# A new order list for the first fourteen steps of an attention and two-layer kernel, with two halves scaled on another engine and a split last tile

## The chip, the cores and the metric

The kernel runs on one core of a Trainium2 chip. The metric is the time of one execution on the device, in microseconds. The core has five engines that work side by side, each with its own queue of instructions that it takes in order: PE (TensorE, matrix products), DVE (VectorE), ACT (ScalarE), POOL (GpSimd) and SP (SyncE, which here only issues DMAs). An engine that waits for a semaphore holds up everything behind it in its queue.

## The reference

Attention over local windows and block summaries, and then two dense layers with a rational function between them:

```python
# B, H, S, D = 4, 8, 768, 64; blocks of 32 keys, window of 16
k_sum = k.reshape(B, H, nb, block, D).max(axis=3)
v_sum = v.reshape(B, H, nb, block, D).mean(axis=3)
scores_l = scale * np.matmul(q, k.transpose(0, 1, 3, 2))      # kept where |i - j| < 16
scores_s = scale * np.einsum('bhsd,bhnd->bhsn', q, k_sum) + np.log(block)
a = softmax(concatenate([scores_l_masked, scores_s]))
x = (a @ concatenate([v, v_sum])) as [3072, 512]
h = x @ w_in                                                  # [3072, 2048]
g = (a0 + a1 h + a2 h^2 + a3 h^3) / (1 + |b0| |h| + |b1| h^2 + 1e-6)
out = g @ w_out                                               # [3072, 512]
```

## The kernel before

**Halves.** The queries are cut into 48 "halves" of 64 positions (all 8 heads of one batch); a half sees a window of 96 keys and 24 block sums, 120 columns for each of four pairs of heads. A half goes through a chain of small stages: its key sums are copied beside its keys (DVE, tile `kw`, halves 8, 9, 12 and 13 of the first sixteen), PE makes the scores (`sc`), DVE adds the mask and takes the extreme of each row (`ss`, `sm`), ACT takes four exponentials and their sums, DVE a reciprocal, POOL multiplies the four pairs by it (tile `ss`), PE transposes (`pt`), ACT or DVE copies the transposed tile out (`pts`; `ENG_P` says which), PE multiplies by the values (`av`), ACT or DVE casts the result (`xh`; `ENG_X`) and DVE keeps the rest of the cast (`xl`). `PAIRS` says which neighbours have their scores made in one interleaved run of products. Halves 0 to 7 are the first group's 512 tokens and are all needed before the first dense step; 8 to 15 are the second group's.

**Steps.** Six groups of 512 tokens go through 16 slices of the hidden layer each: 96 steps. A step is 12 products of PE into a bank `h` (first layer, every operand as a high and a low part), the rational function on ACT, DVE and POOL (`gelu`, parts a to k, tiles `ta`, `tq`, `tu`, `gh`, `gl`), and 12 products into the four banks `po` (second layer). `h` and the transposed tiles of early halves share two PSUM banks. Weights arrive packed (`wr`) and are split into a high and a low part in up to six stages `w` over ACT, POOL and DVE; the first eight slices stay in `wearly`.

**The order written out.** Up to step 13 the order of all engines is a text, `TEXT`, of 562 tokens. Each token stands for the next stage of one chain: `h7` the next stage of half 7, `w3` of the splitting of weights 3, `x2` four of step 2's first-layer products, `y2` three of its second-layer products, `ga2` to `gk2` the parts of its rational function, `K`, `k` key loads and key sums of batch 0, `I`, `i` those of batch 1, `Q` queries, `V` value windows, `A` queries and keys of a half, `W` a load of packed weights, `F`, `G` values for the block means, `v`, `u` the products that make the means, `m`, `n` their copies, `S` constants. The class `Kept` ties each instruction to the one before it on its engine, so that every engine runs its instructions in the order in which the text emits them. From step 14 on a loop takes over, in which the framework's own scheduler orders the engines; there every step has its 12 products of each layer, and every fourth step two halves.

**The end.** `finish` copies the four `po` banks of a group out. For the last bank of the last group ACT copies the left half and DVE the right half into one tile `o`, and two DMAs, from ACT's and SP's queues, write it.

Nearly all instructions are emitted through `call` in `Kept`, and so have line 109 in the profile; they are told apart by their tiles.

Of the kernel before, what the change touches and what calls it, by code (L numbers as in the profile page):

```python
# [8 lines left out]
F32 = mybir.dt.float32  # L9
# [4 lines left out]
ALU = mybir.AluOpType  # L14
# [7 lines left out]
NT, DM, DFF = B * S, H * D, 2048  # L22
P = 128
NPAIR = H // 2
# [6 lines left out]
NK = NKW + NB  # L31
# [5 lines left out]
HPG = GT // HQ  # L37
# [7 lines left out]
LAG = 3  # L45
SOFF = 12
NWARM = 6
TEXT = ("K0 K2 k0 K1 Q0 k1 k2 K3 k3 S0 Q1 F0 W0 V0 V1 V2 A9 V3 V5 V6 V7 W1 V4 W2 W3 h0 A8 G0 h0 h0 h1 h1 h0 h3 h1 h2 h0 h4 h6 h1 h2 h4 v0 h5 h0 h1 h1 h3 h4 h2 h0 h3 h6 h2 h2 h0 h2 "
# [11 lines left out]
AVGW = NK + NB - 4  # L60
NLATE = 4
NSTG = 8
# [2 lines left out]
CROSS = 1  # L65
OWN = (0, 1)
NTA = NTQ = NTU = 2
PAIRS = "11001000"
SMODE = "xxxxxxxxxxxxxxxx"
ENG_P = "dddddaadaaaaaaaa"  # L70
ENG_X = "daadaaaaaaadaaaa"
MODE = "ccccceceeccccccc"
SQ_PS = "001001001001110"
PRODUCT = "00000000000000"
TREE = "0000"
KDMA = "00000000"
NHALF = NT // HQ


# [1 line left out]
def tile_kernel(ctx, tc, qw_in, kraw, kwin, vpad, vred, wio, a, b, cmask, cident, cavg, out):  # L81
# [9 lines left out]
    gp = ctx.enter_context(tc.tile_pool(name="gp", bufs=3))  # L91
# [27 lines left out]
    pe, dve, act, gps, syn = (Kept(e) for e in (nc.tensor, nc.vector, nc.scalar, nc.gpsimd, nc.sync))  # L119
# [153 lines left out]
    def softmax(jj, sc):  # L273

        bi, j = divmod(jj, NJ)
        mt = mask[:, 0 if j == 0 else (2 if j == NJ - 1 else 1), :]
        pool, tag = (gp, "gl") if jj < HPG and jj % 2 else (pp, "p")
        ss = pool.tile([P, NPAIR, P], F32, tag=tag, name=f"ss{jj}")[:, :, 0:NK if jj < 2 * HPG else P]
        sm = sp.tile([P, 2, NPAIR], F32, tag="sm", name=f"sm{jj}")
        for pr in range(NPAIR):  # L280
            dve.tensor_tensor_reduce(
                out=ss[:, pr, 0:NK], in0=sc[:, pr * NK:(pr + 1) * NK], in1=mt, op0=ALU.add, op1=ALU.min,
                scale=-SCALE, scalar=3.0e38, accum_out=sm[:, 0, pr:pr + 1])
        yield
        ahead = jj < 2 * HPG and SMODE[jj] == "y"
        if ahead:
            gps.tensor_tensor(ss, ss, sm[:, 0, :].unsqueeze(2).to_broadcast([P, NPAIR, NK]), op=ALU.subtract)
        if jj < 2 * HPG:
            yield
        if ahead:  # L290
            act.activation(ss, ss, AF.Exp, scale=-1.0)
            yield
            dve.tensor_reduce(sm[:, 1, :], ss, axis=AX.X, op=ALU.add)
            dve.tensor_scalar_add(sm[:, 1, :], sm[:, 1, :], 1e-9)
        else:
            for pr in range(NPAIR):
                act.activation(ss[:, pr, 0:NK], ss[:, pr, 0:NK], AF.Exp, scale=-1.0,
                               bias=sm[:, 0, pr:pr + 1], accum_out=sm[:, 1, pr:pr + 1])
            act.activation(sm[:, 1, :], sm[:, 1, :], AF.Copy, bias=1e-9)
            yield  # L300
        dve.reciprocal(sm[:, 1, :], sm[:, 1, :])
        yield
        if jj >= 2 * HPG:
            gps.memset(ss[:, :, NK:], 0.0)
        for pr in range(NPAIR):
            gps.tensor_scalar(ss[:, pr, 0:NK], ss[:, pr, 0:NK], sm[:, 1, pr:pr + 1], 1.0, op0=ALU.mult, op1=ALU.mult)
        att[jj] = ss

# [2 lines left out]
    def half(jj):  # L311

        other = jj ^ 1
        pair = PAIRS[jj // 2] == "1"
        if jj >= HPG:
# [272 lines left out]
    def finish(g, po):  # L588
        for t in range(TPG):
            if g == NG - 1:  # L590
                o = gp.tile([P, DM], F32, tag="gl" if t % 2 else "gh", name=f"o{g}_{t}")
            else:
                o = (gp if t in OWN else pp).tile([P, DM], F32, tag="o" if t in OWN else "p", name=f"o{g}_{t}", bufs=2 if t in OWN else 4)
            if g == NG - 1 and t == TPG - 1:
                rows = out[g * GT + t * P:g * GT + (t + 1) * P, :]
                act.copy(o[:, 0:DM // 2], po[t][:, 0:DM // 2])
                dve.tensor_copy(o[:, DM // 2:], po[t][:, DM // 2:])
                act.dma_start(out=rows[:, 0:DM // 2], in_=o[:, 0:DM // 2])
                syn.dma_start(out=rows[:, DM // 2:], in_=o[:, DM // 2:])
                continue  # L600
            if g == NG - 1 and t % 2:
                dve.tensor_copy(o, po[t])
            else:
                act.copy(o, po[t])
            syn.dma_start(out=out[g * GT + t * P:g * GT + (t + 1) * P, :], in_=o)
# [107 lines left out]
    for step in range(NSTRICT, NG * NFC + LAG):  # L713
        g, fc = divmod(step, NFC)
# [85 lines left out]
```

## Time and profile before

| | us |
|---|---|
| median of 3 runs | 642.72 |
| lowest, highest | 640.96, 643.12 |
| the profiled execution | 643.12 |
| its span from first to last instruction | 641.3 |
| busy in the span: PE, DVE, ACT, POOL | 619.3, 569.2, 459.7, 254.7 |

In lines of the timeline the columns are start and length in us, engine, operation, tile written and tiles read, shapes, count, and in brackets the idle time just before and what ended it. In lines of groups the columns after the count are the total busy time in us and the mean of one in ns, then the idle time before them with its main causes. Matmuls are pipelined, so their lengths overlap: twelve products of 512 columns follow each other in 2.72 us.

### The profile page before, as it was taken

What the parts mean: (1) busy time and instruction counts of PE and PEld (TensorE: products, weight loads), DVE (VectorE), ACT (ScalarE), POOL (GpSimd) and SP (SyncE); (2) the same over time, 40 slices, a digit from 0 to 9 for tenths busy, and PEclk for the clock granted to TensorE, in tenths of its full rate; (3) what the DMA queues carried; (4) which work ended last, traced back from release to release, by engine and by line L of the source; (5) the groups of instructions that cost most, each with busy time, mean ns of one, the idle gap of its engine ahead of it and who ended that gap; (6) DMA issues with size and microseconds to landing.
All of it is one profiled execution on the core that took longest, in us unless ns stands there. A gap on an engine that the chain in (4) does not pass through costs nothing.

```text
span 641.3 us, 11876 instructions
## 1 busy us (share of the span) xinstructions
PE 619.3 (97%) x4068; PEld 495.4 (77%) x4068; DVE 569.2 (89%) x1152; ACT 459.7 (72%) x1032; POOL 254.7 (40%) x353
## 2 busy tenths in 40 slices
PE   8797899999999999999999999999999999999997
PEld 5565667778778887888888878888888888888886
DVE  5689989999989999988988989988988989898884
ACT  3987989978778667777667687676786675755553
POOL 1838567574243244243243234334234232222221
PEclk9998999999999999999999999999999999999999
DMA  9997756604434424333424342322342210100001
GB/s 322 301 351 259 219 169 195 230 26 132 135 136 146 125 86 138 114 130 108 143 83 133 106 151 86 103 90 84 92 151 83 73 64 1 46 20 2 0 2 65
DMA packets 52136, 78.58 MB, mean 123 GB/s; under 512 B 6132, under 2 KB 33396, under 8 KB 50156
## 3 DMA queue, kind: packets, MB, share of 16 engines
q1 hardware_dynamic: 50796, 75.67, 36.0%
q0 software_dynamic: 560, 1.77, 1.5%
q8 instruction: 32, 0.52, 0.4%
q10 hardware_dynamic: 720, 0.38, 0.2%
q14 instruction: 28, 0.23, 0.1%
HBM read 61.31 MB, written 14.73 MB: 119 GB/s over the span
## 4 chain that ended last, share of the span: by engine, by line
PE 46%; DVE 28%; ACT 13%; issue 6%; POOL 5%; DMA 2%; DVEq 0%; ACTq 0%; POOLq 0%
PE po L109 21%; PE h L109 20%; DVE tu L109 9%; DVE tq L109 8%; DVE gh L109 4%; ACT ta L109 4%; POOL ss L109 3%; ACT ss L109 3%; PE sc L109 2%; PE av L109 2%; DVE ss L109 2%; DMA kres<-in_kraw_dram 1%; ACT tu L109 1%; DVE tb L109 1%; DVE ks L109 1%
## 5 line engine op out<-in xcount | busy, mean ns | idle before, releaser
L109 POOL TENSOR_TENSOR gl<-tu,ta 128x512 fp32r<-128x512 f32 x96 | 130.0, 1354 | 300.9 <-DVE tu L109 163.0
L109 ACT ACTIVATE ta<-tq,cs 128x512 f32<-128x512 f32 x96 | 69.6, 725 | 91.7 <-DVE tq L109 91.4
L109 PE MATMUL po<-wearly,gh 128*128 128x512 f32 x384 | 121.1, 397 | 1.0 <-ACT o L109 1.0
L109 POOL TENSOR_SCALAR ss<-ss,sm 128x120 f32<-128x120 f32 x192 | 93.8, 506 | 65.8 <-DVE sm L109 64.7
L109 PE MATMUL po<-w,gh 128*128 128x512 f32 x384 | 119.8, 393 | 0.0
L109 PE MATMUL h<-xh,wearly 128*128 128x512 f32 x384 | 98.3, 395 | 0.5 <-ACT xh L109 0.5
L109 PE MATMUL h<-xh,w 128*128 128x512 f32 x384 | 96.4, 390 | 1.3 <-DVE tu L109 0.7
L109 PEld LDWEIGHTS h<-xh,wearly 128*128 128x128 f32 x384 | 72.3, 189 | 16.7 <-issue 0.7
L109 PEld LDWEIGHTS h<-xh,w 128*128 128x128 f32 x384 | 71.8, 188 | 16.9 <-ACT ta L109 1.1
L109 PEld LDWEIGHTS po<-wearly,gh 128*128 128x128 f32 x384 | 70.4, 188 | 18.6 <-ACT o L109 2.9
L109 DVE SCALAR_TENSOR_TENSOR gh<-tu,cs,ta 128x512 fp32r<-128x512 f32 x96 | 73.3, 763 | 11.7 <-ACT ta L109 1.9
L109 PEld LDWEIGHTS po<-w,gh 128*128 128x128 f32 x384 | 71.1, 188 | 15.7 <-issue 1.3
L109 ACT ACTIVATE ss<-ss,sm 128x120 f32<-128x120 f32 x192 | 73.3, 386 | 11.2 <-DVE sm L109 11.0
L109 PE MATMUL po<-wearly,gl 128*128 128x512 f32 x192 | 74.9, 390 | 0.0
L109 PE MATMUL po<-w,gl 128*128 128x512 f32 x192 | 74.8, 390 | 0.0
L109 DVE SCALAR_TENSOR_TENSOR tu<-tu,cs,tq 128x512 f32<-128x512 f32 x96 | 72.3, 753 | 2.7
L109 ACT ACTIVATE tu<-h,cs 128x512 f32<-128x512 f32 x96 | 74.7, 778 | 0.0
L109 DVE SCALAR_TENSOR_TENSOR tu<-tu,cs,h 128x512 f32<-128x512 f32 x96 | 71.1, 740 | 2.2
L109 DVE SCALAR_TENSOR_TENSOR tq<-tq,gh 128x512 f32<-128x512 f32 x96 | 67.4, 702 | 2.8
L109 ACT ACTIVATE ta<-h,cs 128x512 f32<-128x512 f32 x96 | 65.3, 680 | 3.7 <-POOL gl L109 3.5
L109 DVE TENSOR_TENSOR tu<-tu,h 128x512 f32<-128x512 f32 x96 | 64.9, 676 | 1.2 <-ACT tu L109 0.7
L109 ACT ACTIVATE ta<-ta 128x512 f32<-128x512 f32 x96 | 60.7, 633 | 2.7
(76 smaller groups left out, 905.5 us busy)
## 6 DMA issues: line engine op xcount, KB each, us to landing
wr<-in_wio_dram SPq DMA_DIRECT2D x15, 1024.0 KB
cross<-tb SPq DMA_DIRECT2D x32, 256.0 KB
vw<-in_vpad_dram SPq DMA_DIRECT2D x42, 192.0 KB
kw<-in_kwin_dram SPq DMA_DIRECT2D x40, 192.0 KB
pts<-cross SPq DMA_DIRECT2D x96, 64.0 KB
out_dram<-o SPq DMA_DIRECT2D x23, 256.0 KB
qw<-in_qw_dram SPq DMA_DIRECT2D x40, 128.0 KB
kr<-in_kraw_dram SPq DMA_DIRECT2D x12, 384.0 KB
```

The costliest lines, as they stand in the source:

```text
L109: out = getattr(self.engine, name)(*args, **kw)
```

## The change

It puts another text in place of `TEXT`, with the same 562 tokens in another order, and changes five settings and two places of code.

- `PAIRS`: halves 6 and 7 make their scores in one run too.
- `SMODE`: half 1 goes the way "y": POOL subtracts the extreme from all four pairs in one instruction, ACT takes one exponential over 480 columns, DVE sums it and adds the small constant; its four scalings stay on POOL. Halves 3 and 5 go the new way "z": DVE scales all four pairs in one product with the reciprocal broadcast, in place of POOL's four.
- `ENG_P`: the transposed tiles of halves 5 and 14 are copied by DVE instead of ACT. `ENG_X`: half 3's cast goes from DVE to ACT, half 10's from ACT to DVE.
- `KDMA`: half 12's key sums are copied by a DMA from SP's queue instead of by DVE (the other mark in the text stands at half 11, which copies none).
- The last output tile's right half gets a tile of its own.

```diff
-PAIRS = "11001000"
-SMODE = "xxxxxxxxxxxxxxxx"
-ENG_P = "dddddaadaaaaaaaa"
-ENG_X = "daadaaaaaaadaaaa"
+PAIRS = "11011000"
+SMODE = "xyxzxzxxxxxxxxxx"
+ENG_P = "ddddddadaaaaaada"
+ENG_X = "daaaaaaaaaddaaaa"
...
-KDMA = "00000000"
+KDMA = "00011000"
...
-        for pr in range(NPAIR):
+        if jj < 2 * HPG and SMODE[jj] == "z":
+            dve.tensor_tensor(ss, ss, sm[:, 1, :].unsqueeze(2).to_broadcast([P, NPAIR, NK]), op=ALU.mult)
+        for pr in range(NPAIR) if jj >= 2 * HPG or SMODE[jj] != "z" else ():
             gps.tensor_scalar(ss[:, pr, 0:NK], ss[:, pr, 0:NK], sm[:, 1, pr:pr + 1], 1.0, op0=ALU.mult, op1=ALU.mult)
...
+                o2 = gp.tile([P, DM], F32, tag="gh", name=f"o{g}_{t + 1}")
                 act.copy(o[:, 0:DM // 2], po[t][:, 0:DM // 2])
-                dve.tensor_copy(o[:, DM // 2:], po[t][:, DM // 2:])
+                dve.tensor_copy(o2[:, 0:DM // 2], po[t][:, DM // 2:])
                 act.dma_start(out=rows[:, 0:DM // 2], in_=o[:, 0:DM // 2])
-                syn.dma_start(out=rows[:, DM // 2:], in_=o[:, DM // 2:])
+                syn.dma_start(out=rows[:, DM // 2:], in_=o2[:, 0:DM // 2])
```

Of the order itself, engine by engine, the places of which the prediction speaks (a number after a point is the stage of the chain; in a half's chain .1 is the scores, .5 the reciprocal, .6 the scaling, .7 the transposes, .8 the copy, .9 the product with the values, .10 the cast, .11 the rest of the cast; in `w` .0 is ACT's conversion, .2 DVE's combine, .4 DVE's subtraction):

```
PE, before:  ... h4.1 h6.1 v0 h5.1 h0.7 v1 v2 v3 h7.1 v4 v5 h3.7 h2.7 h1.7 h0.9 ...
PE, after:   ... h4.1 h6.1 (and half 7) v0 h0.7 v1 h5.1 v2 v3 h3.7 v4 v5 h2.7 h0.9 h1.7 ...
PE, before:  ... x5 y2 y2 y2 h10.7 y2 h10.9 x6 x6 x6 h12.1 y3 x7 y3 h11.7 ...
PE, after:   ... x5 y1 y2 x6 y2 x6 y2 x6 h10.7 h10.9 y2 y3 x7 x7 h12.1 y3 h11.7 ...
ACT, before: ... h7.4 h2.10 h1.10 h5.8 w1.0 h5.10 h6.8 h4.10 h6.10 h7.10 w1.3 w2.0 w3.0 ga0 ...
ACT, after:  ... h7.4 h2.10 h1.10 w1.0 h3.10 h5.10 h6.8 h4.10 w2.0 h7.10 h6.10 w1.3 ga0 gb0 w2.3 w3.0 ...
DVE, before: ... ge1 gc1 gf1 h8.5 i0 w3.4 gi1 w4.2 ge2 gc2 gj1 i1 h9.5 gf2 w4.4 gi2 w5.2 h8.11 gj2 ...
DVE, after:  ... ge1 gc1 w3.4 gf1 h8.5 i0 gi1 ge2 w4.2 gc2 gj1 h9.5 gf2 i1 w4.4 w5.2 gi2 h8.11 gj2 ...
DVE, before: ... h10.5 i3 h9.11 w6.4 gi4 w7.2 gj4 h12.0 ge5 gc5 gf5 h11.5 h10.11 w8.2 gi5 gj5 ...
DVE, after:  ... h10.5 i3 w6.4 gi4 h9.11 gj4 w7.2 ge5 gc5 h11.5 gf5 h10.10 h10.11 w8.2 gi5 gj5 ...
SP, before:  K0 K2 K1 Q0 K3 Q1 F0 W0 V0 V1 V2 A9 V3 V5 V6 V7 W1 V4 W2 W3 A8 G0 W4 W5 A10 I0 W6 A11 ...
SP, after:   Q0 K2 K1 K0 K3 Q1 F0 W0 A9 V2 V1 V0 V5 W1 V3 W2 V4 V6 V7 W3 A8 G0 W4 W5 I0 W6 A11 A10 ...
```

More of the change, by code (lines that the diff above doesn't have):

```diff
@@ L47 @@
 NWARM = 6
-TEXT = ("K0 K2 k0 K1 Q0 k1 k2 K3 k3 S0 Q1 F0 W0 V0 V1 V2 A9 V3 V5 V6 V7 W1 V4 W2 W3 h0 A8 G0 h0 h0 h1 h1 h0 h3 h1 h2 h0 h4 h6 h1 h2 h4 v0 h5 h0 h1 h1 h3 h4 h2 h0 h3 h6 h2 h2 h0 h2 "
[11 rows of a table removed]
+TEXT = ("Q0 K2 K1 K0 k2 K3 k1 k0 k3 S0 Q1 F0 W0 A9 V2 V1 V0 V5 W1 h1 h0 V3 W2 V4 V6 h0 V7 W3 h0 h1 A8 h0 h1 h0 h3 h1 h4 h0 h2 G0 h6 v0 h4 h2 h1 h3 h4 h2 h2 h2 h3 h1 h6 h0 h2 h3 v1 "
[11 rows of a table added]
 AVGW = NK + NB - 4
```

22 rows, old and new, of the table TEXT are left out of this document.

## The prediction

> **What bounds the kernel now.** I read three views in this order: the page's slices, the busy time in five stretches, and the idle rows of the timeline.
>
> ```profile
> span 641.3 us, 11876 instructions
> ...
> DVE  5689989999989999988988989988988989898884
> ```
>
> ```profile
> 8.70:36.60 27.90, 22.80 (x428) 17.04 (x428) 19.52 (x94) 21.91 (x86) 19.73 (x41) 1.00 1.04 338
> 36.60:145.60 109.00, 100.60 (x646) 75.13 (x647) 103.40 (x200) 95.86 (x191) 67.70 (x64) 0.98 0.60 197
> 145.60:168.00 22.40, 21.70 (x96) 17.59 (x94) 21.73 (x47) 16.44 (x41) 9.14 (x13) 1.00 0.40 119
> 168.00:630.00 462.00, 459.52 (x2856) 376.89 (x2857) 417.88 (x806) 322.42 (x713) 156.61 (x231) 1.00 0.29 90
> 56.20:59.60 3.40, 3.40 (x10) 2.63 (x9) 3.37 (x5) 3.31 (x10) 1.90 (x2) 0.50 0.86 335
> ```
>
> The columns are stretch, length, then busy time of PE, PE weight loads, DVE, ACT and POOL, the granted clock, the DMA share and GB/s. After 168 us PE is busy 459.52 of 462.00 us: that part is PE's own work, which the change leaves alone, so at most 2.5 us is to be had there. From 36.6 to 168 us DVE is the fullest engine, 103.40 of 109.00 and then 21.73 of 22.40 us. Before 36.6 us nobody is full (19.73 to 22.80 of 27.90 us) and the DMA engines are (share 1.04). So the list can win in two ways: let the first step start earlier, or take idle time out of DVE before 168 us. The next rows say why DVE, and not PE, is the clock to read.
>
> ```profile
> 36.63 0.50 PE L109 MATMUL h<-xh,wearly 128*128 128x512 f32 x1 [0.47 <-ACT xh L109]
> 55.07 0.33 PE L109 MATMUL pt<-ident,ss 128*120 128x128 f32 x1 [2.82 <-POOL ss L109]
> 80.87 0.33 PE L109 MATMUL pt<-ident,ss 128*120 128x128 f32 x1 [1.50 <-POOL ss L109]
> 168.10 0.28 PE L109 MATMUL av<-pts,vw 120*64 120x64 f32 x2 [0.80 <-DVE tu L109]
> ```
>
> PE loses 2.82 us to half 8's scaling and 1.50 us to half 10's, but at 168.10 us it stands again for DVE, 0.80 us. What PE wins earlier and DVE does not, it waits away there. I therefore add up what the change does to DVE until 168 us, plus the tail.
>
> **Part a: the start of the first step, -1.0 us.** The first product (x0, 36.63) waits for ACT's last cast of the eight early halves.
>
> ```profile
> 20.64 1.13 ACT L109 ACTIVATE wr<-wr 128x1024 f32<-128x1024 f32 x1 [0.41 <-DMA wr<-in_wio_dram]
> 24.30 1.06 ACT L109 COPY vw<-vf 24x512 f32<-24x512 f32 x2 [0.79 <-PE vf L109]
> 34.59 0.84 ACT L109 CAST xh<-av 128x256 fp32r<-128x256 f32 x2 [0.34 <-PE av L109]
> 36.20 0.37 ACT L109 CAST xh<-av 128x256 fp32r<-128x256 f32 x1 [0.78 <-PE av L109]
> ```
>
> ```profile
> L109 POOL TENSOR_TENSOR gl<-tu,ta 128x512 fp32r<-128x512 f32 x96 | 130.0, 1354 | 300.9 <-DVE tu L109 163.0 <-ACT ta L109 47.8 <-ACT ss L109 27.2
> ...
> L109 ACT ACTIVATE wr<-wr 128x1024 f32<-128x1024 f32 (+1 forms) x17 | 18.4, 1095 | 0.4 <-DMA wr<-in_wio_dram 0.4
> L109 DVE TENSOR_TENSOR xl<-x,xh 128x512 fp32r<-128x512 f32 x16 | 10.9, 682 | 0.0
> L109 ACT COPY pts<-pt 120x512 f32<-120x512 f32 x10 | 5.9, 585 | 3.4 <-PE pt L109 3.4
> L109 ACT CAST xh<-av 128x256 fp32r<-128x256 f32 x13 | 4.7, 367 | 5.2 <-PE av L109 5.1
> L109 DVE COPY pts<-pt 120x512 f32<-120x512 f32 x6 | 4.1, 680 | 1.5 <-PE pt L109 1.5
> L109 DVE COPY kw<-ks 128x96 f32<-128x96 f32 x8 | 1.6, 232 | 0.0
> L109 DVE CAST xh<-av 128x256 fp32r<-128x256 f32 x3 | 1.3, 422 | 0.5 <-PE av L109 0.5
> ```
>
> Half 1's new path takes ACT from nine instructions to one, but ACT then only waits longer for weights 0, which land at 20.64 whatever stands before: the bytes ahead of them in SP's queue are the same. I give that nothing. Pairing halves 6 and 7 moves half 7's score products from ahead of the last two v tokens to half 6's place, so the 0.79 us at 24.30 goes. ACT gives half 5's copy to DVE (0.585) and gets half 3's cast (0.367): -0.22. The conversion of weights 2 (1.095) comes before the last two casts, where ACT waited 0.34 and 0.78 for PE: covered, and 1.1 us dearer if those waits have gone too. Sum -0.79 - 0.22 = -1.0.
>
> ```profile
> 22.08 1.23 DVE L109 SCALAR_TENSOR_TENSOR wr<-wr 128x1024 int32<-128x1024 int32 x1 [1.63 <-POOL wr L109]
> 24.74 0.28 DVE L109 CUSTOM_DVE_ANT_0 ss<-sc,mask 128x120 f32<-128x120 f32 x1 [1.44 <-PE pt L109]
> 51.01 0.93 DVE L109 TENSOR_REDUCE ks<-kr 128x24 f32<-128x768 f32 x1
> ```
>
> DVE pays for this. Two products of 480 elements at 682 x 480/512 = 0.64 us each, for half 1 a reduction and an addition (0.93 x 480/768 = 0.58 and about 0.2 us), half 5's copy 0.680, less half 3's cast 0.422: +2.3 us. The cover is DVE's waits of 1.63 us for the first weights and of 1.44 us ahead of half 7's scores, which the pairing brings forward.
>
> POOL loses eight scalings and gains one subtraction ahead of half 0's scaling, priced like POOL's product of 512 elements (1.354 x 480/512 = 1.27 us); half 0's transposes stand behind a v product, which hides most of it. The key-sum copy that becomes a DMA waits in SP's queue for a sum long made; only weights 11 stand behind it: nothing. In the same queue weights 1 pass four value windows and half 11's load passes half 10's; none of the idle rows above is for any of these, so nothing, and at worst the slower rival's way in.
>
> **Part b: half 8, -1.1 us.**
>
> ```profile
> 30.52 2.75 POOL L109 TENSOR_SCALAR ss<-ss,sm 128x120 f32<-128x120 f32 x8 [0.21 <-DVE sm L109]
> 51.51 4.19 POOL L109 TENSOR_SCALAR ss<-ss,sm 128x120 f32<-128x120 f32 x4
> ```
>
> ```profile
> 50.92 0.18 DVE L109 RECIPROCAL sm<-sm 128x4 f32<-128x4 f32 x1
> ...
> 51.85 1.22 DVE L109 TENSOR_TENSOR wearly<-wr,wearly 128x1024 fp32r<-128x1024 f32 x1
> 52.98 0.75 DVE L109 SCALAR_TENSOR_TENSOR gh<-tu,cs,ta 128x512 fp32r<-128x512 f32 x1
> 53.64 1.23 DVE L109 SCALAR_TENSOR_TENSOR wr<-wr 128x1024 int32<-128x1024 int32 x1
> 63.86 0.42 DVE L109 TENSOR_TENSOR xl<-av,xh 128x256 fp32r<-128x256 f32 x1 [1.11 <-ACT xh L109]
> 85.48 0.42 DVE L109 TENSOR_TENSOR xl<-av,xh 128x256 fp32r<-128x256 f32 x1 [0.85 <-ACT xh L109]
> 87.72 0.75 DVE L109 SCALAR_TENSOR_TENSOR gh<-tu,cs,ta 128x512 fp32r<-128x512 f32 x1 [0.68 <-ACT ta L109]
> ```
>
> Eight scalings of halves 6 and 7 take 2.75 us, four of half 8 take 4.19, while DVE runs three instructions on SBUF operands back to back (51.85 to 54.87). The Trainium skill, "SBUF — State Buffer", section "Who interferes with whom", says that a DVE instruction with two SBUF inputs and a GpSimd one that reads SBUF exclude each other for the whole instruction; by that rule these rows agree, and the new products of halves 3 and 5 would hold POOL up too. In the new list weights 3's subtraction (1.22) stands before the reciprocal and weights 4's combine behind a gelu product that reads PSUM. The reciprocal comes at 51.0 - 1.0 + 1.2, about 51.2; the key sum runs beside two scalings, only gh (0.75) blocks, and the last is out some 2.1 us later, at 53.4 instead of 55.7. Half 8's residue on DVE then no longer waits 1.11 us. If the four stay at 4.19 us, this term is 0.
>
> **Part c: halves 10 and 11, -0.8 us.** The same waits at 85.48 and 87.72 us, 0.85 + 0.68 = 1.53. Half 9's residue now splits the two blocking instructions behind half 10's reciprocal from the third, and step 6's products stand ahead of half 10's transposes. I take half, for ACT's order changes as well. Ends 0 and -1.5.
>
> **Part d: DVE's later extras, +0.9 us.** Half 10's cast 0.422 and half 14's copy 0.680, less one key copy 0.232. DVE has no idle time there to hide them.
>
> **Part e: the tail, -0.4 us.**
>
> ```profile
> 636.91 1.11 ACT L109 COPY o<-po 128x512 f32<-128x512 f32 x2 [0.77 <-PE po L109]
> ```
>
> ```profile
> 638.04 0.42 DVE L109 COPY o<-po 128x256 f32<-128x256 f32 x1 [1.13 <-ACT o L109]
> ```
>
> DVE's half of the last tile starts when ACT's ends (638.02), though they touch different columns. With a tile of its own it waits for PE alone and ends 0.4 us earlier, level with ACT's. Bounds 0 and -0.4.
>
> **Sum.** -1.0 - 1.1 - 0.8 + 0.9 - 0.4 = -2.4 us. The profiled execution took 643.12 us for a span of 641.3; it gives 640.7. It was the slowest of three, 0.4 over their median 642.72, so I say 640.3 for a median. A difference under 0.3% (1.9 us) can't be told from none here.
>
> **The rivals.**
> *No change.* The start comes 1.0 us earlier, but POOL's scalings are caught between DVE's instructions as before, and b and c are 0: -1.0 + 0.9 - 0.4 = -0.5, 642.2 us. For it: DVE is full, 95%, and any order leaves POOL few gaps. The clock fits in here: at 56.20 to 59.60 us PE ran at 0.50 after standing still. The new list has the same transposes ahead of the same step, so PE can stand as long and pay the 0.50 again; by the Trainium skill, "TensorE: Matmul & The Clock Gate", section "What's actually happening", one idle window of about 3.4 us is enough.
> *Slower.* DVE's early waits stay, as they are for a DMA, ACT and PE, and the +2.3 us come on top: x0 late by 2.3, b and c 0: +2.3 + 0.9 - 0.4 = +2.8, 645.5 us. It decides if x0 starts after 36.63 us, where it starts now. Against it: 27.90 - 19.52 = 8.4 us of idle DVE in that stretch.
> *More.* b and c in full (2.6) and half of DVE's other 109.00 - 103.40 - 2.6 = 3.0 us idle: -1.0 - 2.6 - 1.5 + 0.9 - 0.4 = -4.6, 638.1 us. For it: PE gets work ahead of three of its waits.
>
> **How the numbers follow.** Forecast 0.40, more 0.15, no change 0.27, slower 0.18. Faster by over 0.3% is 0.40 + 0.15 = 0.55, within 0.27, slower 0.18. The forecast's own range is 639.0 to 640.8. For 8 in 10 I go from 637.0, past the centre of "more", to 645.0, which leaves out about half of "slower" and the lowest of "more".
>
> **What would show it.** Right: x0 near 35.6; four scalings of half 8 in about 2 us; no wait of DVE for half 8's cast; PE's wait near 166 us no longer than 0.8; the last two copies side by side. Wrong: x0 after 37, or DVE's idle time from x0 to the loop not below 5.6 us, or PE's wins handed back in longer waits for DVE between 140 and 170 us.

## The result, and the profile after

The kernel after takes 648.05 us (median of 8 executions, 644.65 to 649.35) against 643.05 (640.96 to 645.10) for the kernel before on the same chip: ratio 1.0069, interval 1.0044 to 1.0094. It is slower, and outside the forecast's range. Its profiled execution took 645.55 us, one of its two quickest, so the page shows less than the median lost. First that page: the span, VectorE's busy tenths in 40 slices of 16 us, and the granted clock in the same slices.

```profile
span 643.8 us, 11870 instructions
...
DVE  5689999999989999988988989988988988898885
...
PEclk9899999999999999999999999999999999999999
```

The span is 2.5 us longer. The first digit of the clock that isn't 9 stands in the second slice (16 to 32 us) and not, as before, in the fourth. The same stretches as in the prediction, cut at the new start of the first step and at 147.0 us in place of 145.6 (the listed `y10` ends 1.3 us later), and two stretches of 3.4 us:

```profile
8.70:39.80 31.10, 24.42 (x428) 16.86 (x428) 22.70 (x98) 21.51 (x79) 18.19 (x34) 0.95 1.04 337
39.80:147.00 107.20, 98.73 (x646) 73.84 (x647) 103.55 (x200) 93.83 (x188) 67.08 (x63) 1.00 0.59 192
...
168.00:630.00 462.00, 458.33 (x2852) 375.59 (x2851) 417.08 (x806) 322.21 (x712) 155.74 (x232) 1.00 0.29 91
18.60:22.00 3.40, 3.40 (x8) 1.40 (x6) 2.00 (x11) 2.89 (x11) 2.12 (x4) 0.50 1.11 266
56.20:59.60 3.40, 2.22 (x9) 1.48 (x10) 3.40 (x7) 3.37 (x13) 3.11 (x5) 1.00 0.98 363
```

What is lost is lost before the first step: 31.10 us of attention where there were 27.90. From there to the end of the listed part it is 107.20 us (109.00 before), with 3.65 us of idle VectorE (5.60 before), so this part looks as the forecast wanted it. But the profile before has a stretch at half clock in this part, at 56.20 us, and this one has not; without half clocks the old list takes no longer there, as is shown below. At 18.60 us PE is busy all of 3.40 us at 0.50.

PE's rows with idle time, from seven places of the timeline:

```profile
15.04 0.30 PE L109 MATMUL sc<-kres,qres 64*64 64x96 f32 x2 [0.88 <-DVE sm L109]
...
17.91 0.31 PE L109 MATMUL sc<-kres,qres 64*64 64x96 f32 x4 [1.85 <-issue]
...
18.31 1.83 PE L109 MATMUL vf<-vf,kres 128*120 128x512 f32 x2
...
39.80 1.42 PE L109 MATMUL h<-xh,wearly 128*128 128x512 f32 x5 [0.47 <-ACT xh L109]
...
56.83 0.67 PE L109 MATMUL pt<-ident,ss 128*120 128x128 f32 x2 [2.19 <-POOL ss L109]
...
101.35 1.20 PE L109 MATMUL h<-xh,w 128*128 128x512 f32 x4 [1.24 <-DMA w<-wr]
...
169.88 1.15 PE L109 MATMUL av<-pts,vw 120*64 120x64 f32 x32 [1.18 <-DVE tu L109]
```

The paired scores of halves 6 and 7 stand still twice. At 15.04 they wait 0.88 us for VectorE, because half 7's bank is the one that half 2's masking has to leave first; at 17.91 they wait 1.85 us for nothing that the profile names ("issue"). The product for the block means behind them (18.31) takes 1.83 us, where the kernel before, at 14.42 us, took 1.12: half clock. (This is one product: those of the scores, of the values and of the means stand in the profile as two records each.) x0 starts at 39.80 instead of 36.63, and at 169.88 us PE stands 1.18 us for VectorE (0.80 before). ScalarE and half 8's scaling in the same profile:

```profile
24.14 0.40 ACT L109 ACTIVATE ss<-ss,sm 128x120 f32<-128x120 f32 x1 [2.61 <-DVE sm L109]
...
27.75 1.06 ACT L109 COPY vw<-vf 24x512 f32<-24x512 f32 x2 [1.76 <-PE vf L109]
...
56.41 1.89 POOL L109 TENSOR_SCALAR ss<-ss,sm 128x120 f32<-128x120 f32 x4 [1.92 <-DVE sm L109]
...
56.14 0.17 DVE L109 RECIPROCAL sm<-sm 128x4 f32<-128x4 f32 x1
```

The wait for the means, 0.79 us before, is 1.76 us now, and 2.61 us for half 5's extremes have come in front of it. Half 8's four scalings take 1.89 us instead of 4.19, but they begin at 56.41 instead of 51.51.

### The profile page after: what moved, and what is told of

It is laid out like the page before. It is cut to its first block, busy times and chain, and to the rows that moved or that the text cites. A ratio compares the mean times of both kernels' runs of the same rounds, so it can differ in the third digit from the quotient of the medians.

```text
span 643.8 us, 11870 instructions
## 1 busy us (share of the span) xinstructions
PE 619.2 (96%) x4068; PEld 493.8 (77%) x4068; DVE 572.4 (89%) x1157; ACT 457.6 (71%) x1022; POOL 252.4 (39%) x346
## 4 chain that ended last, share of the span: by engine, by line
PE 53%; DVE 23%; ACT 10%; POOL 6%; issue 5%; DMA 4%; DVEq 0%; ACTq 0%; POOLq 0%
PE po L109 24%; PE h L109 23%; DVE tu L109 7%; DVE tq L109 7%; POOL ss L109 4%; DVE gh L109 3%; ACT ss L109 3%; ACT ta L109 2%; PE av L109 2%; PE sc L109 2%; DMA w<-wr 1%; DVE ss L109 1%; PE vf L109 1%; POOL gl L109 1%; DVE tb L109 1%
## 5 line engine op out<-in xcount | busy, mean ns | idle before, releaser
L109 POOL TENSOR_SCALAR ss<-ss,sm 128x120 f32<-128x120 f32 x184 | 88.3, 498 | 53.1 <-DVE sm L109 52.0
L109 ACT ACTIVATE ss<-ss,sm 128x120 f32<-128x120 f32 x188 | 71.8, 386 | 14.4 <-DVE sm L109 14.2
```

The source lines that it names most:

```text
L109: out = getattr(self.engine, name)(*args, **kw)
```

## The experiments

Each of them ran beside the kernel before on one chip, and its ratio is against those executions. Each execution also lists its mean granted clock. Over all 369 executions of these kernels, a straight line with one slope and a constant for each kernel (for the kernel before one in each comparison) gives 0.50 us (standard error 0.02) for each 0.001 of mean clock that is missing, and leaves 0.7 us of scatter. A stretch of 3.4 us at 0.50 takes 0.0026 off the mean, so by this slope it costs 1.3 us. "At full clock" below is that constant (standard error 0.1 to 0.3); it tells waits apart from clock. "Missing clock" is 1 less the mean granted clock, averaged over a kernel's executions. The ratio is the one on record with its interval, and not the quotient of the two medians.

| kernel | median us | ratio, interval | missing clock, mean | at full clock | x0 in the profile |
|---|---|---|---|---|---|
| before (five comparisons) | 643.42 to 643.80 | 1 | 0.0033 to 0.0046 | 641.50 to 641.97 | 36.63 |
| after | 648.05 | 1.0069, 1.0044 to 1.0094 | 0.0084 | 643.29 | 39.80 |
| old start, new rest | 644.22 | 1.0018, 1.0004 to 1.0032 | 0.0045 | 642.00 | 36.75 |
| new start, old rest | 645.20 | 1.0017, 0.9999 to 1.0034 | 0.0051 | 642.29 | 40.63 |
| after, 6/7 apart | 646.56 | 1.0041, 1.0021 to 1.0061 | 0.0075 | 642.63 | 39.25 |
| before, 6/7 paired | 646.03 | 1.0044, 1.0023 to 1.0066 | 0.0064 | 643.05 | 39.49 |
| after, 6/7 apart, old loads | 643.22 | 0.9975, 0.9953 to 0.9997 | 0.0038 | 640.92 | 35.74 |
| after, old loads | 645.89 | 1.0043, 1.0024 to 1.0063 | 0.0067 | 643.12 | 39.39 |
| before, new loads | 644.32 | 1.0007, 0.9989 to 1.0025 | 0.0033 | 642.61 | 37.48 |
| before, 11 products | 641.48 | 0.9966, 0.9953 to 0.9980 | 0.0004 | 641.49 | 36.52 |
| before, 4 products | 643.75 | 0.9992, 0.9971 to 1.0013 | 0.0042 | 641.45 | 36.91 |
| after, 8 products | 645.71 | 1.0027, 1.0004 to 1.0051 | 0.0041 | 643.68 | 39.62 |
| after, 8 products, 7 warm-ups | 645.55 | 1.0032, 1.0018 to 1.0046 | 0.0033 | 644.03 | 39.77 |
| both fixes, 8 products | 642.60 | 0.9980, 0.9963 to 0.9996 | 0.0025 | 641.46 | 38.63 |
| the same, old settings of halves 1, 3 and 5 | 642.48 | 0.9980, 0.9962 to 0.9998 | 0.0021 | 641.59 | 38.07 |
| both fixes, 8 products, 7 warm-ups | 641.83 | 0.9978, 0.9961 to 0.9995 | 0.0021 | 641.21 | 35.62 |
| before, 11 products, 7 warm-ups | 641.96 | 0.9973, 0.9958 to 0.9988 | 0.0005 | 641.64 | 37.59 |
| old start, new rest, 8 products | 643.56 | 0.9994, 0.9976 to 1.0012 | 0.0018 | 642.64 | 36.76 |
| before, split last tile | 644.09 | 1.0013, 0.9999 to 1.0026 | 0.0046 | 641.80 | 36.57 |
| new start with both fixes, old rest, 11 products | 639.70 | 0.9946, 0.9929 to 0.9962 | 0.0008 | 639.36 | 35.93 |

**Which half of the list.** The list was cut at x0: the old part with the new rest, and the other way round. The settings of halves 0 to 7 go with the start, the others with the rest, and both have the split last tile.

```diff
 # old start, new rest
-PAIRS = "11011000"
-SMODE = "xyxzxzxxxxxxxxxx"
+PAIRS = "11001000"
+SMODE = "xxxxxxxxxxxxxxxx"
```

> The list of before up to the first product of step 0 with its settings for halves 0 to 7, and the new list and settings from there on. Theory 1 (the loss is made before the first step, where the paired scores of halves 6 and 7 hold PE's queue, and PE then runs at half clock): x0 near 36.6 us, 642 to 643.5 us beside 643 of before. Rival (the loss is made after the first step, by the order of steps 0 to 13): 646 to 648 us.

> The new list up to the first product of step 0 with its settings for halves 0 to 7, and the list and settings of before from there on. Theory 1: x0 near 39.5 us, 646 to 648 us. Rival (order after the first step): 642 to 643.5 us.

The two ratios are alike, but not their profiles: the old start keeps x0 at 36.75, the new one makes it 40.63. Neither ratio makes up 1.0069, nor do both together; what the two halves do to each other stays open. Both times also lie outside what was expected, 644.22 above 642 to 643.5 and 645.20 below 646 to 648. What is lost before x0 is lost by the new start, and part of it is clock: at full clock the new start with the old rest is at 642.29. Its profiled execution, its slowest, shows how far that can go, 10.20 us in a row at 0.50:

```profile
11.60:21.80 10.20, 9.24 (x171) 7.76 (x172) 6.76 (x58) 6.45 (x31) 4.72 (x12) 0.50 1.05 347
```

**The pair of halves 6 and 7.** It was undone in the kernel after, and done alone in the kernel before.

```diff
-PAIRS = "11011000"
+PAIRS = "11001000"
```

> The changed kernel with halves 6 and 7 unpaired again: half 7's scores stand at their own token, behind v5. Theory 1: x0 between 36.6 and 38 us, 643 to 645 us. Rival 2 (the extra work of halves 1, 3 and 5 on DVE): x0 stays near 39.8 us and the time at 647 to 648 us.

> The kernel before with halves 6 and 7 paired, and nothing else. Theory 1: half 6's token waits on PE for the bank that half 2 or 3 frees, x0 1 to 3 us later, 644.5 to 647 us. Rival 2 (the DVE settings): no change, 643 us.

In the kernel before, the pair alone moves x0 from 36.63 to 39.49 and costs 1.3 us at full clock and 1.4 us of clock. Its PE rows show the same two halts as the kernel after:

```profile
14.71 0.30 PE L109 MATMUL sc<-kres,qres 64*64 64x96 f32 x2 [0.82 <-DVE sm L109]
...
17.45 0.31 PE L109 MATMUL sc<-kres,qres 64*64 64x96 f32 x4 [1.71 <-issue]
...
17.86 2.00 PE L109 MATMUL vf<-vf,kres 128*120 128x512 f32 x2
```

Undone in the kernel after, though, the pair gives x0 only 0.55 us back. Its PE rows say what is late next:

```profile
35.00 0.69 PE L109 MATMUL av<-pts,vr 120*64 120x64 f32 x16 [1.33 <-DMA vr<-in_vpad_dram]
36.81 1.98 PE L109 MATMUL av<-pts,vlast 120*64 120x64 f32 x32 [1.12 <-DMA vlast<-in_vpad_dram]
39.25 3.78 PE L109 MATMUL h<-xh,wearly 128*128 128x512 f32 x8 [0.46 <-ACT xh L109]
```

```profile
36.20:43.00 6.80, 5.73 (x41) 4.80 (x42) 5.34 (x8) 2.74 (x4) 1.14 (x1) 0.50 1.05 396
```

The products of halves 4 and 7 with their values wait 1.33 and 1.12 us for the value windows `vr` and `vlast`, which the new list queues behind weights 1 and 2 in SP's queue; and that idle time takes the clock to 0.50 for 6.8 us.

**The order of the early loads.** The head of SP's queue, up to `G0`, was put in the old order, with the pair undone and with the pair kept; and in the kernel before the 15 tokens from `W0` to `G0` were put in the new order.

```diff
 # after, SP's queue
-Q0 K2 K1 K0 K3 Q1 F0 W0 A9 V2 V1 V0 V5 W1 V3 W2 V4 V6 V7 W3 A8 G0
+K0 K2 K1 Q0 K3 Q1 F0 W0 V0 V1 V2 A9 V3 V5 V6 V7 W1 V4 W2 W3 A8 G0
```

> The kernel after with two parts undone: halves 6 and 7 each make their own scores, and the first 26 loads of SyncE's queue (keys, queries, weight blocks, value windows) go in the order of the kernel before; every other engine keeps the new list. Theory (the pair costs the early part, the value windows behind W1 and W2 cost the end of the attention): x0 starts at 35.6 to 36.7 us instead of 39.25 with the pair alone undone, no wait over 0.5 us on a value window before x0, and 642.0 to 644.5 us. Rival (the new list of the compute engines is slow by itself, whatever the loads do): x0 stays after 38.5 and the time at 646 to 647.

> The kernel after with the first 26 loads of SyncE's queue in the order of the kernel before, and nothing else changed: the pair of halves 6 and 7 stays. Theory (the pair alone holds TensorE by about 3 us): x0 at 38.3 to 39.6, values of half 4 no longer waiting for a load, 645.5 to 648. Rival (the loads were the main cost): x0 before 37.5 and 642 to 644.5.

> The kernel before with the new order of its 15 early loads of weights, windows and average inputs, from W0 on (V3, V4, V6, V7 behind W1 and W2, half 9's load ahead of the windows), and nothing else. Theory: values of halves 4 and 7 wait 0.7 to 1.5 us for their windows, x0 at 37.5 to 38.7 instead of 36.63, and 644.5 to 646.5 us. Rival (TensorE is late enough there anyway that the windows land in time): x0 within 0.4 of 36.63 and the time within 0.7 of the kernel before.

With both undone x0 starts at 35.74 us and no load is waited for from the values on:

```profile
33.98 1.28 PE L109 MATMUL av<-pts,vlast 120*64 120x64 f32 x32 [0.33 <-DVE pts L109]
35.74 1.45 PE L109 MATMUL h<-xh,wearly 128*128 128x512 f32 x5 [0.47 <-ACT xh L109]
```

Either one alone leaves x0 almost where it was: 39.25 without the pair, 39.39 with the old loads. With the pair PE is so late that the windows have landed; only without it do they become the last thing that PE waits for. The kernel before agrees, against my expectation: with the new loads its x0 is 0.85 us late, but the rows ahead of x0 have the waits of the kernel before. The delay is made at the "issue" wait: PE comes there 0.35 us later than before and waits 1.46 us instead of 0.97.

```profile
36.33 0.69 PE L109 MATMUL av<-pts,vlast 120*64 120x64 f32 x16 [0.46 <-DVE xl L109]
37.48 1.89 PE L109 MATMUL h<-xh,wearly 128*128 128x512 f32 x7 [0.47 <-ACT xh L109]
```

No value window is waited for, and the ratio can't be told from 1.

**The clock at half 8.** PE got products whose result nobody reads, into the bank of half 8's transposed tile and ahead of the transposes: 11 or 4 in the kernel before, 8 in the kernel after.

```diff
+        for k in range(11 if jj == 8 else 0):
+            pe.matmul(pt, weights(0)[:, 0, 0, 0:P], x32[0][0][:, 0, :], start=True, stop=True)
         for pr in range(NPAIR):
```

> The kernel before with 11 products of 128x512 whose result nobody reads, placed on TensorE ahead of half 8's four transposes, where it waited 0.37 and 2.82 us for the scaling; all else is the same, and so is the output. Theory (that idle stretch takes the granted clock down for 3.4 us, which costs about 1.3 us): no window at 0.50 between 50 and 62 us, mean granted clock over 0.998 in most executions, 641.6 to 642.6 us. Rival (the clock falls for another reason, or the idle stretch is only moved): a window at 0.50 stays there and the time is that of the kernel before, or 0.5 us above it.

> The kernel before with 4 products instead of 11 ahead of half 8's transposes, so that TensorE is still idle there for about 1.5 to 2 us. Theory (the clock falls when a stretch of 3.4 us is busy less than about half; with 4 products it is busy about 80%): as with 11, mean clock over 0.998 and 641.3 to 642.4 us. Rival (any idle of 1.5 us or more can bring it): mean clock 0.996 to 0.998 in most executions and 642.8 to 643.8 us.

> The kernel after, complete, with 8 products of 128x512 that nobody reads ahead of half 8's transposes. Theory (only part of its low clock comes from this place; the wait of the paired scores at 15 to 18 us takes the clock down too): 646.0 to 647.3 us, mean clock 0.994 to 0.997, x0 still near 39.8. Rival (all its low clock comes from this place): mean clock 0.998 or more and 643.3 to 644.3 us.

Eleven products that do nothing make the kernel before 2.3 us faster (641.48 against 643.78 of the same comparison). Its mean clock goes to 0.9996. By the slope 1.7 of the 2.2 us between the means are clock; the 0.5 us left is about twice its error. PE's rows with 11 and with 4:

```profile
50.97 3.11 PE L109 MATMUL pt<-xh,wearly 128*128 128x512 f32 x11
53.92 0.38 PE L109 MATMUL pt<-ident,ss 128*120 128x128 f32 x2
55.02 0.67 PE L109 MATMUL pt<-ident,ss 128*120 128x128 f32 x2 [0.72 <-POOL ss L109]
55.46 1.15 PE L109 MATMUL h<-xh,wearly 128*128 128x512 f32 x4
```

```profile
51.33 1.49 PE L109 MATMUL pt<-xh,wearly 128*128 128x512 f32 x4
52.66 0.27 PE L109 MATMUL pt<-ident,ss 128*120 128x128 f32 x1
53.58 0.32 PE L109 MATMUL pt<-ident,ss 128*120 128x128 f32 x1 [0.64 <-POOL ss L109]
55.40 0.67 PE L109 MATMUL pt<-ident,ss 128*120 128x128 f32 x2 [1.50 <-POOL ss L109]
```

With 11 one wait of 0.72 us is left, and 12 executions miss 0.0004 on average. With 4, 0.64 and 1.50 us are left; this profiled execution kept its clock, but 10 of the 12 show 0.997 or less, and the time is that of the kernel before. I had expected 4 to be enough, because a stretch of 3.4 us there would be busy some 80%; that fell. The rule behind it, that the clock falls after a stretch that is busy less than half, didn't: it depends on where the stretch lies, as the last section shows. The kernel after gets 2.2 us of clock from its 8 products (missing clock 0.0084 to 0.0041), but not the rest.

**The other two places.** The seventh warm-up product keeps PE busy until the first keys are there; it was tried with the kernel after, with the kernel that has both fixes, and with the kernel before as a control.

```diff
-NWARM = 6
+NWARM = 7
```

> The new list with halves 6 and 7 apart and the first 26 loads in the old order (643.22 us, 0.9975 of before), and 8 products of 128x512 that nobody reads ahead of half 8's transposes, where TensorE waited 2.19 us. Theory (the two fixes are independent: earlier start and rest at equal clock -0.9, no half-clock window -1.7): 640.2 to 641.5 us, mean clock over 0.998 in most executions, below both kernels and below the kernel before with products alone (641.48). Rival (the fill pays only where the wait was 2.82 us, and the low clocks of this list come from elsewhere): mean clock stays about 0.996 and the time 642.5 to 643.5.

> The new list with halves 6 and 7 apart, the old order of the first 26 loads and the 8 products ahead of half 8 (642.60 us, mean clock 0.9975), and 7 instead of 6 warm-up products on TensorE at the start, so that it isn't idle before the first scores, where its profile shows a wait of 1.10 us and then a granted clock of 0.71 at 10 to 14 us. Theory (the idle before the first scores is the second place that takes the clock down in this list): mean clock over 0.9985 in most executions and 641.0 to 642.0 us. Rival (the seventh product delays the first scores by up to 0.6 us and the low clock comes from elsewhere): mean clock 0.996 to 0.998, 642.5 to 643.5 us.

> The kernel after, complete, with the 8 products ahead of half 8 (645.71 us, mean clock 0.996) and 7 warm-up products instead of 6. Theory (its third place, the wait of the paired scores at 15 to 18 us, stays): a window at 0.50 near 18 to 22 us in the profile, mean clock 0.996 to 0.998, 645.0 to 646.3 us. Rival (the start's idle was the whole rest): mean clock over 0.9985 and 643.5 to 644.3 us.

> The kernel before with 11 products ahead of half 8's transposes (641.48 us, mean clock 0.9996) and 7 warm-up products instead of 6: the control for the seventh product. Theory (its clock has nothing left to lose, so the product only delays the first scores where the loads came early): 641.4 to 642.2 us, mean clock over 0.999. Rival (a few executions still lose clock at the start): 641.0 to 641.4.

The kernel with both fixes and 8 products came to 642.60 us and not to the 640.2 to 641.5 expected. In its profile PE waited 1.10 us for keys ahead of its first scores and 0.59 us for key sums at 11.59, and lost the clock right after; the columns of the second line are again those of the stretches:

```profile
9.66 0.40 PE L109 MATMUL sc<-kres,qres 64*64 64x96 f32 x8 [1.10 <-DMA kres<-in_kraw_dram]
```

```profile
11.40:14.80 3.40, 3.21 (x86) 3.21 (x88) 2.27 (x21) 1.85 (x10) 1.04 (x2) 0.55 1.06 390
```

With seven warm-ups PE isn't idle there, but the ratio stays as it was (0.9978 against 0.9980): no gain of the seventh product is shown. Another wait shows, 2.16 us at step 8, which every profile with the new rest has (1.24 to 2.58 us; with the old rest it is 0.63 us at most but for the new start with the old rest, 1.66):

```profile
98.01 2.08 PE L109 MATMUL h<-xh,w 128*128 128x512 f32 x4 [2.16 <-DMA w<-wr]
```

```profile
98.00:101.40 3.40, 3.39 (x8) 2.75 (x9) 0.37 (x1) 1.28 (x3) 1.79 (x4) 0.52 0.89 296
```

The new list issues the DMA that adds the remainder of weights 8 some 1.6 us earlier (93.8 instead of 95.4 us), but it takes longer to land. The three lines are from the view of DMA issues that write the tile `w` at 84 to 104 us, for the kernel before, the kernel after, and this one:

```profile
DMA to landing us min/median/max: 5.9/5.9/5.9
```

```profile
DMA to landing us min/median/max: 7.5/7.5/7.5
```

```profile
DMA to landing us min/median/max: 8.4/8.4/8.4
```

With the new start and the old rest it takes 7.0 us. Why it differs wasn't tried. In the kernel after, 8 products and 7 warm-ups leave one low stretch, the one behind the paired scores:

```profile
18.40:21.80 3.40, 3.40 (x12) 1.87 (x8) 1.52 (x10) 3.34 (x15) 2.73 (x6) 0.53 1.11 272
```

The control loses about 0.2 us at full clock, within the error. So the kernel after can lose clock behind the paired scores and at half 8; that some of its executions also lose it at the first scores or at step 8 is inferred from the profiles of kernels near it.

**The new settings, the rest of the list and the tail.** The old way of normalising was put back for halves 1, 3 and 5 (half 4's is the same in both lists); the old start with the new rest got its 8 products; the split tile was put alone into the kernel before; and the parts that paid were put together.

```diff
 # both fixes, 8 products, old settings
-SMODE = "xyxzxzxxxxxxxxxx"
+SMODE = "xxxxxxxxxxxxxxxx"
```

> As the kernel with both fixes and the 8 products, and the normalising of halves 1, 3, 4 and 5 done as in the kernel before: no product by VectorE for halves 3 and 5, no subtraction by GpSimd with sum by VectorE for halves 1 and 4; the list is unchanged. It prices the new settings alone. Theory (the settings free ScalarE and GpSimd early, where x0 waits for ScalarE): x0 0.5 to 2.0 us later than with them, the time 0.3 to 1.5 us longer. Rival (VectorE's extra 2.3 us cost more than they free): x0 earlier, the time shorter by 0.3 or more.

> The old list and settings up to the first product of the first layer and the new list behind it (644.22 us), with 8 products that nobody reads ahead of half 8's transposes. With the clock's share out of the way it prices the new list behind step 0 alone (the terms for halves 8 to 11, VectorE's later extras and the tail, forecast at -1.4 us together) against the kernel before with 11 such products (641.48). Theory (these terms came to nothing): 641.3 to 642.3 us at a mean clock over 0.998. Rival (the forecast -1.4 is there and was hidden by the clock): 639.9 to 640.7.

> The kernel before with the last output tile as two tiles, and nothing else. Theory from four profiles (VectorE's copy still stands behind ScalarE's, and from its end to the end of the span it takes 3.3 us with two tiles, 2.8 with one): VectorE's wait for ScalarE stays at 1.1 us, end of the span 3.2 to 3.4 us after the end of VectorE's last copy, the time within 0.8 of the kernel before and not faster. Rival (the two copies run side by side once the tiles differ, as forecast): VectorE starts within 0.2 us of ScalarE and the time is 0.4 less; the 3.3 us come from the list instead.

> The parts that paid, together: the new list and settings up to step 0 with halves 6 and 7 apart and the first 26 loads in the old order, the old list, settings and tail behind it, and 11 products of 128x512 that nobody reads ahead of half 8's transposes. Theory (the start is worth 0.8 to 1.0 us at full clock, the new list behind it and the tail cost): x0 at 35.6 to 36.5, mean clock over 0.999, 640.4 to 641.2 us, below the kernel before with the products alone (641.48). Rival (VectorE is full from step 0 on, so an earlier start is waited away before 147 us): 641.3 to 642.0.

These three settings are worth nothing that can be measured: 642.48 without, 642.60 with them, and x0 half a us earlier without them, not later. The other new settings stayed in. The new rest costs 0.2 us at full clock against the old one without products (642.00 and 641.78 in one comparison) and 1.2 with them (642.64 and 641.49 in two, with an error of 0.3 between them). With the new start and both fixes it costs 2.1 (641.46 with the new rest and 8 products, 639.36 with the old one and 11). It saves nothing in any of them. The split tile changes nothing: VectorE's copy waits for ScalarE's as before, in the kernel after and in the kernel before with the split alone.

```profile
639.67 0.37 ACT L109 COPY o<-po 128x256 f32<-128x256 f32 x1 [0.17 <-PE po L109]
...
640.07 0.42 DVE L109 COPY o<-po 128x256 f32<-128x256 f32 x1 [1.16 <-ACT o L109]
```

```profile
636.59 1.11 ACT L109 COPY o<-po 128x512 f32<-128x512 f32 x2 [0.77 <-PE po L109]
...
637.73 0.42 DVE L109 COPY o<-po 128x256 f32<-128x256 f32 x1 [1.13 <-ACT o L109]
```

The profiles had suggested another price for it: from the end of VectorE's last copy to the end of the span it is 3.24 to 3.35 us in the eleven profiles with the new rest, and 2.80 to 2.89 us in the nine with the old one. The split alone has 2.85, so those 0.45 us belong to the list and not to the tile. What makes them stays open.

The last kernel takes the new start with both fixes, the old rest and tail, and 11 products: 639.70 us, ratio 0.9946 (0.9929 to 0.9962), the fastest of all and quicker than expected (640.4 to 641.2). Its x0 comes 0.59 us earlier than that of the kernel before with 11 products; where the rest of the difference to 641.48 comes from wasn't traced. It rests on 6 executions.

```profile
35.93 2.11 PE L109 MATMUL h<-xh,wearly 128*128 128x512 f32 x8 [0.47 <-ACT xh L109]
```

## Why the prediction was wrong

**The start (term a, -1.0).** This step failed: +3.17 us in the profiled execution. It says that pairing "moves half 7's score products from ahead of the last two v tokens to half 6's place, so the 0.79 us at 24.30 goes". I looked at what the move takes away and not at what it puts in front of everything else on PE: 16 more products (32 records) at 13.8 us, for which a second PSUM bank must be free (VectorE, 0.88 us) and behind which v0 and half 0's transposes queue, with 1.85 us of "issue" and a half clock on top. The pair alone, in the kernel before, makes x0 2.86 us late. The kernel before has an "issue" wait at the same place of PE's stream, 0.97 us at 17.17, but there v0 is already through.

**SP's queue.** This step, "none of the idle rows above is for any of these, so nothing", failed too. It also counted wrong: by the lists weights 1 pass three windows (`V3`, `V6`, `V7`), and weights 2, which it left out, pass `V4` as well. No idle row showed the windows because PE was too late to need them. With the pair gone, PE is about 1 us earlier than in the kernel before (the last product of the means at 22.30 us instead of 23.25), and the same order costs up to 3.5 us (39.25 against 35.74), half clock included.

**The size of term a** came out once both were undone: x0 at 35.62 to 35.93 in the three profiles with both fixes that kept their clock at the start, 35.63 forecast. But it came out without the pair, which was the reason given: with halves 6 and 7 apart, half 7's scores stand behind the last v token in the new list, and that takes ScalarE's 0.79 us away. In the two profiles in which the clock fell behind the first scores x0 is 38.07 and 38.63.

**VectorE's extra 2.3 us** cost nothing in the time, as forecast: without 2.1 of them (the old way of halves 1, 3 and 5) it is the same.

**Half 8 (b, -1.1).** The mechanism was right and the size wrong. The four scalings shrank from 4.19 us to 1.89, 1.89 to 1.91 in every profile with the new rest and 3.92 to 4.19 with the old. But the reciprocal ahead of them came 16.3 us after x0 instead of 14.3, where the sum had allowed 1.2 us for it. So x0 to the start of step 3, the same products in both, takes 18.66 us instead of 19.22, and two profiles with the new start and the old rest are as short (18.70 and 18.73). **Halves 10 and 11 (c, -0.8):** PE's wait of 1.50 us for half 10's scaling is gone; 0.65 us for weights and 0.68 us for a copy stand near there instead. **VectorE's extras (d, +0.9)** weren't priced by themselves. **The tail (e, -0.4)** is 0: the step that failed is "with a tile of its own it waits for PE alone". The two copies read one PSUM bank, and the program still lets VectorE wait for ScalarE's semaphore. The Trainium skill, "PSUM — Partial Sum Buffer", section "PSUM bank collisions raise a hardware error", says that two engines must not access one bank at once in the same partitions, reads among them; the rows agree with a program that keeps to this, and no run here tried it otherwise.

Terms b to e, -1.4 us together, came to between +0.2 and +2.1. Two profiles without a half clock while PE works show where they went: "after, 6/7 apart, old loads" beside "before, 11 products".

| stretch | before, 11 products | after, 6/7 apart, old loads | difference |
|---|---|---|---|
| to x0 | 36.52 | 35.74 | -0.78 |
| x0 to x3 | 18.94 | 18.69 | -0.25 |
| x3 to x12 | 66.29 | 66.63 | +0.34 |
| x12 to the end of the listed y10 | 17.37 | 17.49 | +0.12 |
| y10 to PE's last product | 496.33 | 495.93 | -0.40 |
| PE's last product to the end of the span | 3.75 | 4.22 | +0.47 |

Between x3 and x12 the list wins and gives back: its wait for weights at step 8 is 1.44 us instead of 0.56. Only the start is earlier and only the end later by much; the 0.40 us behind y10 say nothing, for that stretch varies by 1.1 us between the profiles. Where the wait at step 8 takes the clock with it, it costs 1.3 us more by the slope; the old start with the new rest and 8 products shows 0.997 in 6 of 12 executions, and its profile 0.50 from 99.7 to 103.1 us.

**The rivals.** "Slower" has the sign and names the point at which it decides, x0 after 36.63. Its mechanism, VectorE's extra work, isn't the one. "No change" names the half clock at 56 us, and that "PE can stand as long and pay the 0.50 again". I gave it no price in the sum; the runs give it about 2 us, in the kernel before as well. So the forecast's base was one that could be beaten by 2.3 us without any change to the list. Of the 3.8 us between the means of the kernel after (647.5) and of the kernel before over all five later comparisons (643.7), about 1.5 are at full clock and 2.3 are missing clock (0.0084 against 0.0039, times 504). On the chip of the result itself the means are 4.4 us apart, and the clocks of the kernel before aren't on record there.

**Wrong criteria.** "x0 after 37" told it at once. VectorE's idle time from x0 on, 3.65 us, said "right" while the time was lost elsewhere, so the step "why DVE, and not PE, is the clock to read" failed as well: from x0 to the end of y10 the two profiles of the table take 102.60 and 102.81 us.

## What to carry to other kernels

When products are moved ahead of others in an in-order queue, price what now stands behind them, and what they need that was free at their old place (here a bank), before counting the wait that they leave. A load that nobody waits for is hidden only at the present pace: make the consumer 1 us faster and look again. Where PE waits 1.5 us or more between products, a handful of products that nobody reads can be worth more than a reordering: fill until PE is busy for more than half of any 3.4 us, wherever they begin.

## What the runs showed of the hardware

In each profile the granted clock changes between 1.00 and 0.50 on a grid of 3.41 us, which lies differently from profile to profile. Cut along this grid, the 20 profiles say when the clock falls (PE's busy time as the profile has it, from 4 to 635 us). All 18 stretches at full clock in which PE was busy less than 0.497 of the time were followed by one at 0.50. Of the five with 0.50 to 0.515 two were, and of some 3,600 above that one, with 0.58. So it is not the length of one wait that decides, but how much of one stretch of the grid is idle:

```profile
52.80:56.20 3.40, 1.10 (x5) 0.67 (x6) 3.40 (x6) 3.35 (x10) 3.31 (x4) 1.00 0.94 314
...
52.71:56.13 3.42, 1.94 (x7) 0.93 (x5) 3.42 (x4) 3.36 (x12) 1.69 (x2) 1.00 0.95 318
56.13:59.54 3.41, 2.16 (x9) 1.42 (x10) 3.41 (x7) 3.38 (x12) 3.05 (x5) 1.00 0.99 361
...
52.32:55.73 3.41, 1.26 (x6) 0.47 (x4) 3.41 (x5) 3.36 (x6) 3.37 (x3) 1.00 0.87 267
...
24.24:27.65 3.41, 2.04 (x28) 1.52 (x26) 2.37 (x12) 3.38 (x9) 2.97 (x6) 1.00 1.02 309
```

The first line is half 8 in the kernel before, 1.10 of 3.40 us busy, and the clock falls behind it. In the kernel after an edge of the grid at 56.13 us cut the wait of 2.19 us in two; both stretches are more than half busy, and the clock stayed. The last two lines are the emptiest 3.41 us anywhere in the profiles with 4 and with 11 products. With 4 it is busy 1.26 us, if the grid happens to lie there, and 10 of 12 executions paid; with 11 it is busy 2.04 us, and none of 12 did. A wait is thus paid in some executions and not in others, and it is the emptiest stretch that has to be filled.

The Trainium skill, "TensorE: Matmul & The Clock Gate", section "Why this matters for your kernels", asks for no idle gaps over about 3 us between bursts of products; by these runs, in which waits of 1.07 and 1.50 us close together were paid for, that is too generous, and the measurement decides. Its section "What's actually happening" lets the clock go by a window that runs freely, and a grid that lies differently from profile to profile agrees with this.

The "issue" wait belongs to a place in PE's stream. It is the 222nd record of a product that waits, also with a seventh warm-up product, which shifts the program's products by two records. It does so in the 13 profiles in which the record before it starts ahead of 17 us: 0.70 to 0.99 us in the kernels that make the old list's start, 1.46 with the new loads in it, and 1.49 to 1.85 with the pair, which brings PE there at 15.5 to 16.2 us. No profile starts that record before 17.05 us, and the seven that come to it later don't wait. Between 8 and 20 us one transfer of the queue for instructions is on record, here for the kernel after (queue and kind, packets, MB, share):

```profile
q8 instruction: 1, 0.02, 0.6%
```

That PE waits for its instructions there fits both; it was not tried by itself. It also says what the pair did: it put the product for the means, on which ScalarE and the values depend, behind this place instead of ahead of it.
